# A fused LayerNorm, sliding-window attention and gated-FFN kernel: PV products per pair of head groups with resident attention weights and the first FFN weights on ScalarE's queue, in place of PV for four groups per run with streamed attention weights

## The chip, the cores and the metric

The kernel runs on one core of one Trainium2 chip. The metric is device time in microseconds for one launch of the whole program; the time before is the median of three runs.

## The reference, cut to what matters

```python
xn = (x - mean) / sqrt(var + 1e-5)                 # x: 1 x 2048 x 576, bf16
q, k, v = split(xn @ wqkv)                         # 32 heads of 18
mask = 0 <= i - j < 256                            # causal, window of 256
s = softmax(where(mask, q k^T * 18**-0.5, -1e9)) v # per head
s = s @ wo                                         # 576 x 576
h = sigmoid(xn @ w_gate) * (xn @ w_up)             # w_gate, w_up: 576 x 4608
g = h @ w_down                                     # 4608 x 576
out = x + s * silu(g)
```

## The kernel before, in words

The 2048 tokens are cut into four chunks of 512 (`NC = 4`), and each chunk into four blocks of 128 tokens. For a chunk the program normalizes x, brings it into the layout with features on partitions (`xnT`), projects V (`build_v`) and Q, K (`build_qk`, five column groups), does attention for eight head groups of four heads (`build_attn`), projects with `wo`, and does the FFN (`build_ffn`). The contraction over 576 features is 64 + 4 x 128; all matmuls use two halves of the array's rows, so they come in pairs that run side by side (`pair`, line 133).

In an attention step the scores of a head group fill five tiles ("bins") of 1024 columns. ScalarE takes exp of each into one slot of the ring `expr`, VectorE multiplies the mask blocks, and later a **PV run** (`f_pv` in `build_pv`, line 838) multiplies the weights with V. A PV run consists of matmuls that load 19 columns of V (18 and a column of ones for the softmax sum) and stream 64 to 320 columns; eight of them, four on the column groups times two on the row halves, run side by side. With `PVG = 2` a run serves four head groups: 192 matmuls (128 in chunk 0, which has no keys of an earlier chunk), eight runs in all. The `expr` ring has `NEX = 20` slots, which is what four head groups need. VectorE then transposes, divides by the sums and transposes back, and DMAs put the result in `oT`.

The attention weights are not kept: `load_qk` brings the columns of each Q/K group again in every chunk into a ring of two (`wqk`, `wqkr`), and `load_proj` brings `wv` and `wo` in turn into one buffer (`wvo`, `wvor`). The gate and up weights come from HBM in every chunk too, in 18 groups of two tiles of 128 hidden features, into a ring of four (`wgs`, rows 64 to 575) and a ring of two (`wgr`, the first 64 rows). `w_down` is loaded once.

The order on every engine is fixed when the program is built: `schedule` takes operations one after the other by estimated start and priority, so that FFN matmuls fill TensorE while attention steps wait for ScalarE and VectorE. TensorE executes its list in order. All loads are issued from SyncE (SP); the moves within SBUF from POOL and SP. `SPACE_NS` holds, for each chunk and head group, the distance in time that the planner keeps between the score tiles.

TensorE's list also contains waits. A matmul carries one semaphore wait itself; further ones stand in the list as instructions of their own. In `pad_pe` the program counts TensorE's instructions, compares the place of each PV run with a period of 256 instructions, and writes extra waits for something long done into the FFN steps ahead of it:

```python
            phase = (sizes[i][0] + added + PHASE) % HALF
            mid, lo = PV_PHASE[0], PV_PHASE[1] - PV_PHASE[0]
            need = 0 if (phase - mid) % HALF <= lo else (mid - phase) % HALF
```

At the start SyncE issues four loads of x, the first gate and up weights (`dma:w:0:0`), their first 64 rows, and then the next groups, while TensorE multiplies zeros (`warm`) and ScalarE loads its table (`init:tab`, line 481).

Of the kernel before, what the change touches and what calls it, by code (L numbers as in the profile page):

```python
# [36 lines left out]
NEX = 20  # L37
NWQ = 2
PVG = 2
# [15 lines left out]
          ((3, 1, 1, 2), (7, 1, 0, 1)), ((4, 1, 1, 2),))  # L55
NXN = 2
NST = 3
NQD = 1
NFIN = 2
NTH = 4  # L60
OT_PRIO = 1
EVAC = (1, 0)
NOT1 = 1
NOT2 = 1
NOT3 = 2
MK_PRIO = 1
# [15 lines left out]
HALF = 256  # L82
PHASE = 73
PV_PHASE = (80, 124)
WAITS_FREE = 2
# [11 lines left out]
SPACE_NS = ((2200, 1700, 1500, 1700, 1700, 1700, 1700, 2000),  # L97
            (1700, 2200, 1300, 1500, 2500, 1600, 1700, 900),
            (1600, 1200, 1700, 2000, 900, 1700, 1300, 1700),
            (2200, 1700, 1700, 2200, 1700, 2500, 1700, 700))  # L100
# [4 lines left out]
def mm_ns(n):  # L105
    return max(24.7, n / 2.4 + 2.7)
# [42 lines left out]
class Hold:  # L149

    __slots__ = ("pool", "n", "units", "rel", "parts")

    def __init__(self, pool, n):
        self.pool = pool
        self.n = n
        self.units = None
        self.rel = []
        self.parts = None
# [3 lines left out]

    def split(self):
        self.parts = [Hold(self.pool, 1) for _ in range(self.n)]
        return self.parts


class Pool:
# [27 lines left out]
    def take(self, hold, units):  # L196
        deps = []
        for u in units:
            if self.last[u] is not None:
                deps += self.last[u].rel  # L200
            self.last[u] = hold
        hold.units = units
        for u, part in zip(units, hold.parts or ()):
            self.last[u] = part
            part.units = [u]
        return deps
# [40 lines left out]


class Counter:

    def __init__(self):
        self.n = 0

    def matmul(self, *a, **k):
        self.n += 2

    transpose = matmul
# [22 lines left out]
class Builder:  # L280
# [38 lines left out]
    def alloc_memory(self):  # L319
# [30 lines left out]
        self.ot1, _ = seq("ot1", [P, NOT1, NT], f32)  # L350
        self.o2, _ = seq("o2", [P, NOT2, NT])
        self.o2T, _ = seq("o2T", [P, NOT3, NT])
        self.oT, _ = seq("oT", [P, KB, NT])
        self.s_attn, _ = seq("s_attn", [P, BPC, D])
        self.wqk, _ = seq("wqk", [P, NWQ, KB - 1, 2, P])
        self.wqkr, _ = seq("wqkr", [P, NWQ, P])
        self.wvo, _ = seq("wvo", [P, KB - 1, D])
        self.wvor, _ = seq("wvor", [P, D // 2])
        self.qd, _ = seq("qd", [P, NQD, 2, NT])
        self.xnr, _ = seq("xnr", [P, NXN, XW])  # L360
# [22 lines left out]
    def build_graph(self):  # L383
        self.r_xn = Ring(NXN, "xnr")
# [4 lines left out]
        self.r_wq = Ring(NWQ, "wqk")  # L389
        self.r_wvo = Ring(1, "wvo")  # L390
        self.r_ex = Ring(NEX, "expr")
        self.r_ot1 = Ring(NOT1, "ot1")
        self.r_o2 = Ring(NOT2, "o2")
        self.r_o2T = Ring(NOT3, "o2T")
# [20 lines left out]
        self.xn_slot = {}  # L415
# [23 lines left out]
    def load_x(self, c, i=0):  # L439
# [8 lines left out]
        for _ in range(2):  # L448
            s_, d_ = self.r_xn.produce()
            slots.append(s_)  # L450
            dd += d_
        assert slots[1] == slots[0] + 1
        o = self.dma(self.xnr[:, slots[0]:slots[0] + 2, RD:XW],
# [3 lines left out]
        for j in range(2):  # L457
            self.x_dma[st + j] = (o, self.xnr[:, slots[j], RD:XW])
            self.xn_slot[st + j] = slots[j]
# [9 lines left out]
    def build_consts(self):  # L469
# [15 lines left out]
        self.warm(NWARM[0], z, None, 107)  # L485

# [35 lines left out]
    def build_ln(self, c):  # L522
# [3 lines left out]
        for i in range(BPC):  # L526
# [24 lines left out]
            sn, dn = (self.xn_slot[st], []) if c else self.r_xn.produce()  # L551
# [16 lines left out]
            self.ln_dup = dup  # L568
            self.r_st.release(ss, ap)
# [56 lines left out]
    def load_proj(self, c, w, name):  # L626
        _, d = self.r_wvo.produce()
        o = [self.load_nat(self.wvo[:, :, :], w, f"dma:{name}:{c}", ("wvo",), 6, d)]
        o += self.load_rem(self.wvor[:, :], (w[:, 0:288], w[:, 288:D]), f"dma:{name}r:{c}", ("wvor",), 6, d)
        if c == 0:  # L630
            for x in o:
                x.slack = 5000.0
        return o

    def load_qk(self, c, gi):
        sw, d = self.r_wq.produce()
        n = P if gi < 4 else RD
        cols = [self.wqkv[:, i * D + gi * P:i * D + gi * P + n] for i in range(2)]
        o = []
        for i, w in enumerate(cols):  # L640
            dst = self.wqk[:, sw, :, i, :] if gi < 4 else self.wqk[:, sw, :, 0, i * RD:i * RD + RD]
            o.append(self.load_nat(dst, w, f"dma:wqk:{c}:{gi}", ("wqk", sw, i), 5, d))
        if gi < 4:
            o += self.load_rem(self.wqkr[:, sw, :], cols, f"dma:wqkr:{c}:{gi}", ("wqkr", sw), 5, d)
        else:
            for t in range(2):
                for i in range(2):
                    o.append(self.dma(self.wqkr[ROWS[t], sw, i * RD:i * RD + RD], cols[i][0:RD, :], 2 * RD * RD * 2,
                                      f"dma:wqkr:{c}:{gi}", ("wqkr", sw, t), deps=d, prio=5))
        if c == 0:  # L650
            for x in o:
                x.slack = 2500.0
        return sw, o

    def build_qk(self, c, gi):
        op = self.op
        sw, wdeps = self.load_qk(c, gi)
# [4 lines left out]

        def lhs(r, t, k):
            return self.wqk[r, sw, k - 1, 0 if gi == 4 else t, :] if k else self.wqkr[r, sw, :]
# [4 lines left out]
        pj = self.two("qk", f"{c}:{gi}", n, h, lhs, rhs, [self.op_xnT[c], wdeps, dq], n)  # L669
        self.r_wq.release(sw, pj)  # L670
# [44 lines left out]
    def build_v(self, c):  # L715
        op = self.op
        wdeps = self.load_proj(c, self.wqkv[:, 2 * D:3 * D], "wv")
        xs = c % 2
        for i in range(BPC):
# [5 lines left out]
            vp = self.row_proj("v", st, h, lambda r, k, cols=cols: self.xnT[r, xs, k, cols], self.wvo, self.wvor,  # L725
                               [self.op_xnT[c][i], wdeps, war])
            self.r_wvo.release(0, vp)
# [16 lines left out]
    def build_attn(self, c, hg):  # L744
# [21 lines left out]
        for vi, (specs, groups) in enumerate(zip(bins, masks)):  # L766
# [27 lines left out]
            for g0, ng, m0, m1 in groups:  # L794
# [10 lines left out]
                mk = op("DVE", dve_ns(2 * ng * (m1 - m0) * SW, 2.0), f_mk, f"mk:{c}:{hg}:{vi}:{g0}", deps=[ex, self.op_mask], prio=MK_PRIO)  # L805
# [6 lines left out]
        if hg % (2 * PVG) == 2 * PVG - 1:  # L812
            self.build_pv(c, hg // 2 - PVG + 1)

    def build_pv(self, c, pr):
        op = self.op
        pend, self.pend = self.pend, []
        hp = self.pool_s.hold(PVG)
        hps = hp.split()
# [5 lines left out]
        def f_pv(eng):  # L825
            res = None
            for u, n, ks in [(u, n, ks) for u in range(PVG) for n, ks in enumerate(kss)]:
                outs = self.halves(hps[u], NT)
                q0, q1 = span[ks]
                cols = slice(q0 * SW, q1 * SW)  # L830
                for g, (hg, where, _) in enumerate(pend[2 * u:2 * u + 2]):
# [10 lines left out]
        est = TURN_NS + PVG * sum(mm_ns((b - a) * SW) for a, b in span.values())  # L842
# [5 lines left out]
        for pr, hp, i in [(pr + u, hps[u], i) for u in EVAC for i in range(2)]:  # L848
# [6 lines left out]
            def f_t1(e, i=i, p1=p1, hp=hp):  # L855
                return e.transpose(self.ot1[:, p1, :], self.halves(hp, NT)[i])  # L856
            t1 = op("DVE", dve_ns(NT), f_t1, f"ot:{c}:{pr}:{i}", deps=[pv, d1], prio=OT_PRIO)
            hp.release(t1)
            rc = op("DVE", 255, lambda e, o1=o1: e.reciprocal(o1[:, :, DH], o1[:, :, DH]), f"rc:{c}:{pr}:{i}", deps=[t1], prio=OT_PRIO)
            on = op("DVE", dve_ns(NT // 32 * DH), lambda e, o1=o1, o2=o2: e.tensor_tensor(  # L860
                o2[:, :, 0:DH], o1[:, :, 0:DH], o1[:, :, DH:VH].broadcast_to([P, NT // 32, DH]), ALU.mult),
                f"on:{c}:{pr}:{i}", deps=[rc, d2, self.op_o2z], prio=OT_PRIO)
            self.r_ot1.release(p1, on)
            t2 = op("DVE", dve_ns(NT), lambda e, p2=p2, p3=p3: e.transpose(self.o2T[:, p3, :], self.o2[:, p2, :]),  # L864
                    f"ot2:{c}:{pr}:{i}", deps=[on, d3], prio=OT_PRIO)
# [8 lines left out]
        if pend[0][0] == 0:  # L874
# [17 lines left out]
    def build_wo(self, c):  # L892
        op = self.op
        wdeps = self.load_proj(c, self.wo, "wo")
        last = []
        for i in range(BPC):
# [7 lines left out]
            wo = self.row_proj("wo", qb, h2, lambda r, k, cols=cols: self.oT[r, k, cols], self.wvo, self.wvor,  # L904
                               [self.op_o[c], wdeps, war])
            self.r_wvo.release(0, wo)
# [217 lines left out]
    def schedule(self):  # L1124
# [14 lines left out]
        while nsched < len(ops):  # L1139
# [66 lines left out]
            for s_ in o.succs:  # L1206
# [8 lines left out]
                if remaining[s_.cidx] == 0 and s_.idx < 0:  # L1215
                    enabled[s_.eng].append(s_)
        self.prog = prog
# [4 lines left out]

    def waits_of(self, o, known):
        waits = {}
        for d in o.deps:
            k, v = d.tok
            if waits.get(k, -1) < v:
                waits[k] = v
        out = [(k, v) for k, v in waits.items() if known.get(k, -1) < v]
        known.update(out)  # L1230
        return out

    def pad_pe(self):
        known, at, sizes, free = {}, 0, [], {}
        prog = self.prog["PE"]
        for o in prog:
            cnt = Counter()
            nw = len(self.waits_of(o, known))
            extra = max(0, nw - WAITS_FREE)
            free[o] = max(0, WAITS_FREE - nw)  # L1240
            o.fn(cnt)
            sizes.append((at + extra, cnt.n))
            at += extra + cnt.n
        pads = {}
        added, first = 0, 0
        for i, o in enumerate(prog):
            if not o.name.startswith("pv:"):
                continue
            phase = (sizes[i][0] + added + PHASE) % HALF
            mid, lo = PV_PHASE[0], PV_PHASE[1] - PV_PHASE[0]  # L1250
            need = 0 if (phase - mid) % HALF <= lo else (mid - phase) % HALF
            hosts = [p for p in prog[first:i] if p.name.startswith("f")]
            for n, p in enumerate(hosts):
                k = need * (n + 1) // len(hosts) - need * n // len(hosts)
                if k:
                    pads[p] = k + free[p]
# [95 lines left out]
```

## Time and profile before

| | before |
|---|---|
| median of three runs | 575.99 us (575.91 to 576.23) |
| the profiled execution, its time | 576.23 us |
| its span, first to last instruction | 574.9 us |
| TensorE matmul busy | 556.7 us, 97% of the span |
| VectorE, ScalarE, POOL busy | 331.6, 273.6, 208.4 us |
| mean granted TensorE clock | 0.994 |
| DMA traffic | 75.90 MB, mean 132 GB/s |
| TensorE matmuls | 8342 |

The profiled execution took 1.3 us more than its span, and 0.24 us more than the median of the runs. Busy time of TensorE is that of pipelined matmuls with modelled ends; where it stands still is seen better in the chain of work that ended last, whose pieces the prediction shows.

### The profile page before, as it was taken

To read this page: it belongs to the slowest core of one execution; us is meant where nothing else is said; L and a number is where in the kernel's file an instruction comes from. 1 tells how busy PE (TensorE), PEld (TensorE's weight loads), DVE (VectorE), ACT (ScalarE), POOL (GpSimd) and SP (SyncE) were. 2 spreads that over 40 slices of the span, in tenths; PEclk is the share of its full clock that TensorE was granted. 3 is DMA by queue.
4 is the path that set the end of the run, shared out by engine and by line. 5 is a ranking of instruction groups with operands and counts; after the bars stand their busy time and mean duration, and the time that the engine had idled before them with its cause. 6 is when DMAs were issued, how large, how long until landed. Compare 5 with 4: busy or idle time off the path is not lost.

```text
span 574.9 us, 19878 instructions
## 1 busy us (share of the span) xinstructions
PE 556.7 (97%) x8342; PEld 359.3 (62%) x8342; DVE 331.6 (58%) x792; ACT 273.6 (48%) x383; POOL 208.4 (36%) x360
## 2 busy tenths in 40 slices
PE   8999997999999989999999999989998999999997
PEld 7565443888566544467775555546877755555687
DVE  4466664844867649656856675575263955642123
ACT  4245651443455645672556366534562567333111
POOL 5614441565442413554633355335141530110000
PEclk9999997999999999999999999999999999999999
DMA  8999896432177634752253376536321156271010
GB/s 224 250 289 241 232 229 193 124 72 67 35 174 221 182 109 121 200 145 53 47 144 108 91 192 167 166 100 160 87 76 35 26 149 179 72 205 47 3 43 23
DMA packets 141343, 75.90 MB, mean 132 GB/s; under 512 B 43804, under 2 KB 139388, under 8 KB 141256
## 3 DMA queue, kind: packets, MB, share of 16 engines
q1 hardware_dynamic: 133832, 68.71, 44.7%
q0 software_dynamic: 7424, 5.92, 3.9%
q8 instruction: 68, 1.11, 0.8%
q14 instruction: 19, 0.16, 0.1%
HBM read 63.18 MB, written 2.36 MB: 114 GB/s over the span
## 4 chain that ended last, share of the span: by engine, by line
PE 96%; issue 2%; DMA 1%; SPq 0%; DVE 0%; DVEq 0%
PE ps L133 92%; PE ps L838 3%; DMA wgs<-in_B_w_up_dram 1%; SPq L309 0%; DVE s_attn L1101 0%; DVE thf L1106 0%; PE ps L610 0%; DVE xf L1111 0%; DVEq L1299 0%
## 5 line engine op out<-in xcount | busy, mean ns | idle before, releaser
L133 PE MATMUL ps<-xnT,wgs 64*128 64x512 bf16 (+1 forms) x2400 | 288.8, 370 | 0.8 <-PE ps L133 0.5
L791 ACT ACTIVATE expr<-ps 128x1024 bf16<-128x1024 f32 (+4 forms) x160 | 154.8, 968 | 83.1 <-PE ps L133 82.4
L133 PEld LDWEIGHTS ps<-xnT,wgs 64*128 64x128 bf16 x2400 | 121.0, 94 | 110.2 <-issue 3.6
L133 PE MATMUL ps<-wd_sb,hT 64*128 64x288 bf16 (+2 forms) x2448 | 155.1, 276 | 0.0
L985 ACT ACTIVATE tring<-ps 128x512 bf16<-128x512 f32 x144 | 86.1, 598 | 136.9 <-PE ps L133 120.4
L988 DVE SCALAR_TENSOR_TENSOR hT<-tring,ps 128x512 bf16<-128x512 bf16 x144 | 98.6, 685 | 77.3 <-ACT tring L985 74.9
L133 PEld LDWEIGHTS ps<-wd_sb,hT 64*128 64x128 bf16 x2448 | 117.9, 94 | 23.7
L309 POOL DMA_DIRECT2D qk<-qd x160 | 81.7, 518 | 100.1 <-PE ps L133 55.5
L804 DVE TENSOR_TENSOR expr<-expr,mask 128x128 bf16<-128x128 bf16 (+2 forms) x240 | 64.6, 299 | 76.3 <-ACT expr L791 74.8
L309 POOL DMA_DIRECT2D oT<-o2T x72 | 36.9, 519 | 112.5 <-DVE o2T L864 91.6
L755 POOL TENSOR_SCALAR kx<-kprev,small 128x256 bf16<-128x256 bf16 x64 | 60.2, 951 | 40.1 <-PE ps L133 39.1
L133 PE MATMUL ps<-qk,kx 64*128 64x320 bf16 (+1 forms) x704 | 60.4, 254 | 0.0
L133 PE MATMUL ps<-xnT,wgr 64*128 64x512 bf16 (+1 forms) x300 | 57.3, 369 | 0.0
L133 PEld LDWEIGHTS ps<-qk,kx 64*128 64x128 bf16 x704 | 33.9, 94 | 23.3 <-ACT expr L791 1.1
L856 DVE STREAM_TRANSPOSE ot<-ps 128x512 f32<-128x512 f32 x32 | 22.4, 701 | 30.2 <-PE ps L838 29.9
L133 PE MATMUL ps<-xnT,wqk 64*128 64x512 bf16 (+1 forms) x320 | 38.0, 355 | 0.1
L1091 ACT ACTIVATE thf<-ps 128x576 bf16<-128x576 f32 (+3 forms) x22 | 11.4, 518 | 49.3 <-PE ps L133 49.0
L838 PE MATMUL ps<-expr,v_aug 64*19 64x320 bf16 (+4 forms) x1408 | 20.2, 255 | 12.8 <-issue 12.8
L838 PEld LDWEIGHTS ps<-expr,v_aug 64*19 64x19 bf16 x1408 | 17.2, 86 | 17.4 <-issue 15.6
L759 POOL COPY kprev<-qk 128x256 bf16<-128x256 bf16 x32 | 12.6, 400 | 38.2 <-DVE kx L755 36.9
L755 DVE TENSOR_SCALAR kx<-qk,small 128x512 bf16<-128x512 bf16 x64 | 21.7, 365 | 7.7 <-PE ps L133 4.4
L133 PEld LDWEIGHTS ps<-xnT,wgr 64*128 64x128 bf16 x300 | 16.1, 95 | 15.9 <-issue 0.5
(67 smaller groups left out, 305.8 us busy)
## 6 DMA issues: line engine op xcount, KB each, us to landing
wgs<-in_B_w_gate_dram SPq DMA_DIRECT2D x72, 256.0 KB, 3.6
wgs<-in_B_w_up_dram SPq DMA_DIRECT2D x72, 256.0 KB, 3.9
wd_sb<-in_B_w_down_dram SPq DMA_DIRECT2D x9, 576.0 KB, 6.4
wqk<-in_A_wqkv_dram SPq DMA_DIRECT2D x32, 128.0 KB, 3.1
qk<-qd POOLq DMA_DIRECT2D x100, 36.0 KB, 2.6
wgr<-in_B_w_gate_dram SPq DMA_DIRECT2D x36, 64.0 KB, 2.9
wgr<-in_B_w_up_dram SPq DMA_DIRECT2D x36, 64.0 KB, 3.1
wvo<-in_A_wqkv_dram SPq DMA_DIRECT2D x4, 576.0 KB, 4.6
```

The lines of the kernel that those rows point to most:

```text
L133: res = eng.matmul(outs[i], lhs(ROWS[t], i), rhs(ROWS[t], i), start=start, stop=stop, tile_position=(64 * t, 0))
L309: o = self.op(eng, DMA_ISSUE_NS[eng], lambda e: e.dma_start(dst, src), name, deps, prio, nbytes=nbytes)
L755: return e.tensor_scalar(self.kx[:, sx, pos:pos + n_ // SW, t, :], src.rearrange("p (s k) -> p s k", k=SW), self.half[:, t:t + 1], None, A ...
L759: self.op_kp[hg] = op("POOL", 420, lambda e: e.tensor_copy(self.kprev[:, hg, :], self.qk[:, qs, 1, NT // 2:NT]), f"kp:{c}:{hg}", deps=[kxo ...
L791: return eng.activation(self.expr[:, se, :, lo * SW:NT], self.both(h, NT)[:, :, lo * SW:NT], ACTF.Exp, scale=SM_SCALE)
L804: return eng.tensor_tensor(e_, e_, m_, ALU.mult)
L838: res = eng.matmul(outs[i][p0:p0 + VH, cols], self.v_aug[ROWS[i], o:o + VH], self.expr[ROWS[i], se, t, cols], start=n == 0, stop=n == len( ...
L856: return e.transpose(self.ot1[:, p1, :], self.halves(hp, NT)[i])
L985: th = op("ACT", act_ns(NT), lambda e: e.activation(self.tring[:, st, :], bank(h, 0), ACTF.Tanh, scale=0.5), f"th:{c}:{ft}", deps=[pg, dt_ ...
L988: mu = op("DVE", dve_ns(NT), lambda e: e.scalar_tensor_tensor(self.hT[:, ft, :], self.tring[:, st, :], 1.0, bank(h, 1), ALU.add, ALU.mult) ...
L1091: return e.activation(v2(t)[:, a:b, :], y2()[:, a:b, :], ACTF.Tanh, scale=0.25)
```

## The change

PV runs serve two head groups (96 matmuls, or 64 in chunk 0; sixteen runs), with an `expr` ring of 12 slots. All of `wqkv` and `wo` is loaded once and stays in SBUF (`wqk`, `wqkr`, `wv_sb`, `wo_sb` and their remainders); the last 64 columns of Q and K are copied together by VectorE (`wq4`). x of later chunks has its own ring (`xr`), `qd` has two slots in place of one. The extra waits on TensorE (`pad_pe`) are gone, `SPACE_NS` has other values. After the order is made, the two loads of the first gate/up weight group are taken out of SyncE's list and put into ScalarE's behind the operation that loads its table; all x loads stay on SyncE.

```diff
-NEX = 20
-NWQ = 2
-PVG = 2
+NEX = 12
...
+NXR = 2
...
-NQD = 1
+NQD = 2
...
-HALF = 256
-PHASE = 73
-PV_PHASE = (80, 124)
-WAITS_FREE = 2
...
+        wq, wk, wv = (self.wqkv[:, i * D:(i + 1) * D] for i in range(3))
+        self.op_wqk = [self.load_nat(self.wqk[:, :, i, :], w, "dma:wqk", ("wqk", i), 5) for i, w in enumerate((wq, wk))]
+        self.op_wqk += self.load_rem(self.wqkr[:, :], (wq, wk), "dma:wqkr", ("wqkr",), 5)
...
+        self.op_wv = [self.load_nat(self.wv_sb[:, :, :], wv, "dma:wv", ("wv",), 6)]
...
+        self.op_wqk4 = [op("DVE", 420, lambda e: e.tensor_copy(self.wq4[:, 1:KB, :, :], self.wqk[:, :, :, 512:D]), "init:wq4",
+                           deps=self.op_wqk, prio=2)]
+        for t in range(2):
+            for i in range(2):
+                self.op_wqk4.append(op("DVE", 130, lambda e, t=t, i=i: e.tensor_copy(
+                    self.wq4[ROWS[t], 0, i, :], self.wqkr[ROWS[1 - i], 512:D]), f"init:wq4:{t}{i}", deps=self.op_wqk, prio=2))
...
     def build_qk(self, c, gi):
         op = self.op
-        sw, wdeps = self.load_qk(c, gi)
...
     def build_v(self, c):
         op = self.op
-        wdeps = self.load_proj(c, self.wqkv[:, 2 * D:3 * D], "wv")
...
         self.pend += [(hg, where, ready)]
-        if hg % (2 * PVG) == 2 * PVG - 1:
-            self.build_pv(c, hg // 2 - PVG + 1)
+        if hg % 2:
+            self.build_pv(c, hg // 2)
+        if (c, hg) == (0, 1):
+            pv = self.op_pv[(c, hg)]
+            self.op_wo_w = [self.load_nat(self.wo_sb[:, :, :], self.wo, "dma:wo", ("wo",), 8, [pv])]
...
         def f_pv(eng):
             res = None
-            for u, n, ks in [(u, n, ks) for u in range(PVG) for n, ks in enumerate(kss)]:
-                outs = self.halves(hps[u], NT)
+            outs = self.halves(hp, NT)
+            for n, ks in enumerate(kss):
...
+        first = [o for o in prog["SP"] if o.name == "dma:w:0:0"]
+        for o in first:
+            prog["SP"].remove(o)
+            o.eng = "ACT"
+            o.deps.append(self.op_tab)
+        at = prog["ACT"].index(self.op_tab) + 1
+        prog["ACT"][at:at] = first
...
-    def pad_pe(self):
...
-                for _ in range(pads.get(o, 0)):
-                    eng.wait_ge(self.sem["DVE"], 1)
```

## The prediction, made before the changed kernel ran

> **What bounds the kernel now.** I read the busy shares first: TensorE has 97% of the span, the next engine 58%. So only what TensorE does or waits for counts. The chain of waits in order of time (start, length, what) shows where its time is not work:
>
> ```profile
> 10.54 77.12 PE ps L133 x804
> 87.65 1.69 PE ps L838 x110
> 89.34 3.28 issue
> 92.62 0.54 PE ps L838 x16
> ...
> 209.12 1.55 PE ps L838 x106
> 210.67 2.43 issue
> 213.10 1.02 PE ps L838 x64
> ...
> 216.24 45.69 PE ps L133 x554
> 261.93 2.45 PE ps L838 x167
> 264.38 55.20 PE ps L133 x808
> ```
>
> Outside the PV runs (line 838) TensorE flows for tens of microseconds without a hole. Inside a PV run it stops once, and waits for "issue": nothing that the profile shows. Seven of eight runs have such a stop; the one at 261.93 has none. TensorE's own waits (total, times, longest) show that nothing else is of that size; no load and no other engine holds it for more than 1.0 us:
>
> ```profile
> PE ps L838 <- issue: 12.8, 7, 3.3
> PE ps L133 <- DVE small L480: 1.0, 1, 1.0
> PE ps L133 <- PE ps L133: 0.5, 3, 0.2
> PE ps L610 <- DVE xnr L558: 0.4, 1, 0.4
> PE ps L133 <- DMA wgs<-in_B_w_up_dram: 0.3, 1, 0.3
> ```
>
> What releases the stops? The table of queues (packets, MB, share) has one of kind "instruction":
>
> ```profile
> q8 instruction: 68, 1.11, 0.8%
> ```
>
> That is 16 KB a packet. TensorE's list has 2 x 8342 instructions for matmuls and their weight loads and 753 waits of their own, 17,438 with one more: 68.1 times 256, so a packet is a block of 256 TensorE instructions. I counted through the built program's list up to the first matmul after each stop: it has number 2496, 4288, 6081, 9665, 11201, 13505 and 15041, each time 192 or 193 above a multiple of 256. The stop is the end of a block whose successor has not come. By the trace's packet times TensorE resumes 1.26 to 1.51 us after a packet of q8 has landed, and a packet's fetch begins, late in the kernel, about when TensorE enters the block before. A block of FFN work takes about 11.5 us, so its successor is there in time; a PV run eats 384 instructions in 2.45 us.
>
> How long a successor needs, counted from the entry into the block ahead of it, is shown by the seven blocks that ended in a stop: 7.18, 3.63, 4.79, 3.08, 4.13, 3.52 and 2.62 us, and at most 2.20 us for the run without a stop. The first is in chunk 0, where the DMA share is highest.
>
> One more thing hangs on the first stop. The stages after 86 us (length, TensorE busy and count, the same of PEld, DVE, ACT and POOL, granted clock, DMA share, GB/s):
>
> ```profile
> 86.00:87.50 1.50, 1.50 (x16) 0.55 (x12) 0.87 (x3) 1.33 (x3) 1.46 (x3) 1.00 1.27 237
> 87.50:93.10 5.60, 2.32 (x130) 1.66 (x129) 0.65 (x1) 0.00 (x0) 0.88 (x1) 0.88 1.13 324
> 93.10:99.00 5.90, 5.74 (x31) 1.94 (x30) 4.17 (x8) 0.60 (x1) 0.00 (x0) 0.53 0.33 109
> ```
>
> After the longest stop the granted clock is 0.53 for 5.9 us.
>
> **The change part by part.** *PV runs of half the length.* What a stop costs I take from whole runs. The unstopped run takes 2.45 us. The other five of chunks 1 to 3 take 5.00, 3.29, 4.99, 4.33 and 3.48 (their pieces in the chain), 8.84 us above 5 x 2.45. The two of chunk 0 (5.51 and 3.41) stream three quarters of the columns, so 1.90 us without a stop, and are 5.12 above. Together 13.9 us. The clock: from 93.10 to 99.00 run 28 matmuls of 512 columns; eight of them take 0.86 us before the stop, so 3.0 us at full clock, 2.9 less than they took, of which 0.24 is a wait between the two halves of one FFN tile. That leaves 2.65 us.
>
> These 16.5 us are there to be had. A run in the new kernel has 192 instructions, so a block holding one entirely has 64 others, and those are slow: eight down-projection matmuls take 0.49 us, 31 ns an instruction; ten gate/up matmuls 1.08 us, 54 ns. I walked through the changed program's list for each run's place in its block. Eleven runs begin 110 to 231 instructions after a block's start, so they are cut in two, with many slow instructions in both blocks; these blocks take 5 us and more, against 2.2 to 4.8. Five are almost whole in one block: the second of chunk 0 begins 4 instructions after the block's start, the last of chunk 1 at 35, the first three of chunk 3 at 5, 17 and 33. A run itself will take about 1.4 us (half the unstopped run, and its own start). With 64 others of 31 ns, as at 17 and 33, the block takes 3.4 us; with 54 ns, as at 5 and 35, 4.6 to 4.8. In chunk 0 (128 instructions in the run, 128 of 46 ns on average around it) it takes 7.1. Against the mean delay of the later stops, 3.6 us, two blocks stop for 0.2 us each; with the scatter up to 4.8, 1.4 each, and the chunk-0 one 0.1. I take 1.0 us in all; the ends are 0 and, if all five meet the longest delay and some f2 block mixed with scores is shorter still, 5.5.
>
> *Eight more starts of a run.* Before the run at 261.86 the last sixteen FFN matmuls need 1.07 us instead of 0.98: 0.09 for the switch. The run streams 5120 columns, 2.15 us at the rate of the gate/up pairs (0.42 ns a column), and lasts 0.31 longer. What of this is paid anew in each run, and what goes with the number of matmuls, the trace does not show: 0.09 to 0.40 a run. I take the middle, 0.25: 2.0 us, ends 0.7 and 3.2.
>
> *Resident attention weights.* SP loses 102 of 112 issues (40 wqk, 48 wqkr, 8 wvo, 16 wvor become 10), and 7.8 of 10.4 MB are not moved. TensorE waits for no load after 8 us, so this is worth nothing on the path, and the cover is the whole queue of FFN work. Where it could cost: in chunk 0 the whole of wqk, wqkr and wv, 1.9 MB, now stand on SP ahead of weight group 4. At the 290 GB/s of the first slices they hold it back 6.5 us, to about 21; group 4 is used after eight FFN tiles and four Q/K passes of 0.9 us, at about 27. If that cover were gone, the price would be the lateness, once. The five copies for wq4 are some 1.2 us of VectorE (0.38 for the nearest large row, 0.20 for a small one), beside a VectorE that is 58% busy.
>
> *The ring of 12, the second qd slot, the x ring, the new spacings.* Ten slots serve a pair of groups, so the third score tile of the next pair waits for the PV run. In the new list that tile stands behind the run, and TensorE, which runs its list in order, waits for itself only. Masks must be ready for a PV run earlier than before, as two groups and not four are collected; TensorE's list puts FFN steps between. The trace has 0.24 us for a hole of that kind, three times; I take no change, and 0 to 2 us for the upper end.
>
> *No extra waits.* 533 instructions leave TensorE's list (753 become 220 waits). They cost nothing while the weight load runs ahead; they made blocks end sooner.
>
> *The first weights from ScalarE.* Now SP issues four x loads until 2.61, then gate 2.65 to 3.08 and up 3.13 to 3.64; the up weights land at 7.67 and the first FFN matmul starts at 7.81. ScalarE's table operation ends at 2.29, so gate starts at about 2.35 and up at about 2.85: 0.3 us sooner. On SP the issues behind move up by 1.0 us. On ScalarE the statistics of the third x block wait behind the two issues, until about 3.4; they wait for x until 4.46 anyway. The activation that brings the first block into xnT ends at 7.06 and TensorE's second transpose at 7.57, so no more than 0.3 can be had. I take 0.3; ends 0.6 gained and 0.3 lost, if both queues' packets share the engines and the up half comes no sooner.
>
> [...]
>
> **The sum.** 576.2 (the profiled execution, span 574.9) - 13.9 - 2.65 + 1.0 + 2.0 - 0.3 = 562.3; the median is 0.24 below the profiled execution, so 562.1, and I say 562. The ends: 576.0 - 16.5 + 0.7 - 0.6 = 559.6 and 576.0 - 16.5 + 5.5 + 3.2 + 0.3 + 2 = 570.5, which needs all bad ends at once; two thirds of the way up is 568.
>
> **The rivals.** *The stop belongs to the run, not to the block.* If each PV run stops once whatever its length, 13.9 / 8 = 1.74 us a run, sixteen cost 27.8: 576.0 + 13.9 + 2.0 - 0.3 = 591.6 with the clock loss as now. It decides against the change where the mean stop of the new runs is over (16.5 - 1.7) / 16 = 0.93 us. For it: seven of eight runs have one. Against it: the one without, and the numbers modulo 256. 5%.
>
> *The fetch is later than in the blocks I took.* If delays of 5 to 7 us, as in chunk 0, were met in chunks 1 to 3 too, some eight blocks would stop, for 6 to 12 us: 567 to 574. For it: the 7.18. Against it: none of the later ones is over 4.8, and less DMA traffic remains. 10%.
>
> *The new order has holes of its own*, in chunk 0's loads or at masks: the same 567 to 574, 3%. *The loads on ScalarE bring nothing:* 562.3, within the forecast.
>
> **How the numbers follow.** My forecast, 559 to 567, has 82%; the later or larger stops 13%; the rival above 576, 5%. The range 559 to 568.5 leaves some 15% out. 0.2% (1.2 us) is about what can be told from no change here. Faster by more: 0.94; within: 0.02; slower: 0.04.
>
> **What would show it.** Right: sixteen PV pieces in the chain, most unbroken at about 1.4 us, issue waits at line 838 under 3 us in all, granted clock 1.00 at 90 to 100 us, first FFN matmul near 7.5. Wrong: a stop in most runs, or TensorE waiting for wgs, expr or hT at line 133.

## The result and the profile after

The changed kernel takes 559.84 us (559.55 to 560.22), against 575.95 us before (the median of four runs now): a ratio of 0.9725 (95% interval 0.9708 to 0.9741), some 16 us less. The forecast was 562 us, with a range of 559 to 568.5.

The chain of waits of the changed kernel, in order of time (start, length, what; line 801 is now the PV run, line 122 the other matmuls):

```profile
65.02 0.94 PE ps L801 x64
65.96 22.02 PE ps L122 x228
87.97 0.94 PE ps L801 x64
88.91 23.44 PE ps L122 x288
...
407.58 1.27 PE ps L801 x90
408.85 17.22 PE ps L122 x294
426.07 1.27 PE ps L801 x89
427.34 12.86 PE ps L122 x218
```

The whole chain has sixteen PV pieces, four of 0.94 us in chunk 0 and twelve of 1.27 us after it, none with a stop. (The counts of such a piece are lower than the 96 matmuls of a run, since matmuls that overlap are merged in the chain.) The stage that ran at half clock before, and the queue of instruction blocks together with the new queue of ScalarE (packets, MB, share):

```profile
93.10:99.00 5.90, 5.90 (x64) 2.75 (x60) 5.34 (x14) 3.94 (x5) 2.64 (x6) 1.00 0.43 117
```

```profile
q8 instruction: 66, 1.08, 0.8%
q10 hardware_dynamic: 1056, 0.52, 0.3%
```

The clock there is 1.00, and TensorE is busy all through. The matmuls in the stretch are not the same ones; eight of 512 columns take 1.03 us, where they took 1.89 at half clock (0.50 granted from 91.80 to 98.63 us in the trace before). What is left of TensorE's waits (total, times, longest) and the place of the one that is new:

```profile
PE ps L122 <- DVE small L451: 1.0, 1, 1.0
PE ps L122 <- issue: 0.9, 1, 0.9
PE ps L599 <- DVE xnr L545: 0.8, 1, 0.8
```

```profile
10.61 0.11 PE ps L122 x3
10.72 0.89 issue
11.61 12.79 PE ps L122 x166
```

The new stop of 0.89 us is not in a PV run but at the very start, among the first FFN pieces; the first matmul after it is instruction 449 of the built list, again 193 above a multiple of 256. It is the only stop at a block's end in this execution, and the forecast did not have it.

### The profile page after: what moved, and what is told of

The parts are those of the page before. It is cut to its first block, busy times and chain, and to the rows that moved or that the text cites. A ratio compares the mean times of both kernels' runs of the same rounds, so it can differ in the third digit from the quotient of the medians.

```text
span 558.9 us, 19261 instructions
## 1 busy us (share of the span) xinstructions
PE 552.9 (99%) x8342; PEld 339.8 (61%) x8342; DVE 333.8 (60%) x797; ACT 274.2 (49%) x383; POOL 210.0 (38%) x360
## 3 DMA queue, kind: packets, MB, share of 16 engines
HBM read 55.15 MB, written 2.36 MB: 103 GB/s over the span
## 4 chain that ended last, share of the span: by engine, by line
PE 98%; DMA 1%; DVE 0%; issue 0%; SPq 0%; ACT 0%; POOL 0%; DVEq 0%
PE ps L122 94%; PE ps L801 3%; DMA x<-in_A_x_dram 1%; PE ps L599 0%; SPq L279 0%; ACT tring L586 0%; DVE s_attn L1062 0%; POOL small L533 0%; DVE xnr L541 0%; DVE thf L1067 0%; DVE xf L1072 0%; POOL small L587 0%; DVE xnr L545 0%; DVEq L1234 0%
## 5 line engine op out<-in xcount | busy, mean ns | idle before, releaser
L122 PE MATMUL ps<-xnT,wgs 64*128 64x512 bf16 (+1 forms) x2400 | 282.7, 368 | 1.0 <-issue 0.9
L122 PEld LDWEIGHTS ps<-xnT,wgs 64*128 64x128 bf16 x2400 | 114.1, 94 | 115.6 <-DVE hT L949 1.6
L122 PE MATMUL ps<-wd_sb,hT 64*128 64x288 bf16 (+2 forms) x2448 | 156.7, 276 | 0.0
L122 PEld LDWEIGHTS ps<-wd_sb,hT 64*128 64x128 bf16 x2448 | 112.7, 94 | 28.2
L764 DVE TENSOR_TENSOR expr<-expr,mask 128x128 bf16<-128x128 bf16 (+2 forms) x240 | 63.3, 298 | 61.9 <-ACT expr L751 61.4
L122 PEld LDWEIGHTS ps<-qk,kx 64*128 64x128 bf16 x704 | 31.2, 94 | 21.5 <-ACT expr L751 0.6
L122 PE MATMUL ps<-xnT,wqk 64*128 64x512 bf16 x256 | 32.6, 376 | 0.0
L1052 ACT ACTIVATE thf<-ps 128x576 bf16<-128x576 f32 (+3 forms) x22 | 11.4, 518 | 39.7 <-PE ps L122 39.4
L827 DVE STREAM_TRANSPOSE o2T<-o 128x512 bf16<-128x512 bf16 x32 | 22.7, 711 | 1.0
L637 DVE CAST qd<-ps 128x1024 bf16<-128x1024 f32 (+1 forms) x20 | 22.1, 1111 | 1.5 <-PE ps L122 1.5
L697 ACT ACTIVATE v_aug<-ps 64x288 bf16<-64x288 f32 x32 | 13.1, 408 | 17.3 <-PE ps L122 16.8
```

What stands on the lines that cost most here:

```text
L122: res = eng.matmul(outs[i], lhs(ROWS[t], i), rhs(ROWS[t], i), start=start, stop=stop, tile_position=(64 * t, 0))
L637: return eng.tensor_copy(dst, self.both(h, n))
L697: return eng.activation(dst, src, ACTF.Copy)
L764: return eng.tensor_tensor(e_, e_, m_, ALU.mult)
```

## The experiments

Three questions were open after the result: is it the block or the run that stops, do the resident weights carry a part of the gain, and where does the stop at the start come from.

### Long runs at other places in their blocks

Two kernels keep the long runs of before and change only the extra waits. One counts the waits as the built list has them: a matmul carries one wait itself, the others stand two to an instruction (at the shifted start below, 128 of them are 64 records in the trace).

```diff
-PHASE = 73
-PV_PHASE = (80, 124)
-WAITS_FREE = 2
+EDGE = 193
+PV_AT = (128, 72)
...
+            size.append(cnt.n + max(0, nw) // 2)
...
+                need = (want - (start - EDGE)) % HALF
...
+                        pads[prog[p]] = 2 * (nws[p] // 2 + k) - nws[p]
```

> The kernel before, with its eight long PV runs, but the extra waits ahead of each run are counted as the built list has them, so that a run begins 128 instructions after a block's start in chunk 0 and 72 (once 89) in chunks 1 to 3; a run is then cut into two nearly equal parts by a block's end. Block theory (the stop is the end of a block of 256 instructions whose successor has not come): most stops go or shrink; the shortest blocks are about 2.5 us for two runs amid down-projection matmuls (about 1.1 us of stop each at the mean delay of 3.6 us), 3.3 us for one, 3.9 us and more for the rest. Sum of stops 2 to 4 us, granted clock 1.00 at 93 to 99 us, time 576.0 - 13.9 - 2.65 + 3 = 562.5 us (561 to 564). Run theory (a run of more than some 105 matmuls stops once wherever it stands, a short one does not): stops of 1.5 to 2 us in seven or eight runs, 574 to 577 us.

Measured: 565.54 us (ratio 0.9828, 0.9761 to 0.9894). Six of the eight long runs have no stop. The chain shows an unbroken one, whose 2.40 us are all 192 matmuls, and the one with the longer stop of the two others:

```profile
203.82 2.40 PE ps L837 x164
206.22 2.07 PE ps L132 x17
...
428.02 1.24 PE ps L837 x86
429.26 1.54 issue
430.81 1.42 PE ps L837 x93
```

The run at 428 stands amid down-projection matmuls, one of the two that were expected to stop; its stop is after 92 of 192 matmuls, at the block's end, where it was after 152 before. The other run stops for 0.5 us, and two stops of 0.4 and 0.3 us stand behind a run, each at a block's end too: 2.8 us in all, as expected. So the length of the run does not make the stop, and the run theory is out. The time is 1.5 us above the range given. In the traces the first PV run starts at 89.27 us, against 87.65 in the kernel before, which has 600 wait instructions fewer, and 87.16 in the next kernel, which has no extra waits: the further ones are not free at the start (below).

The other kernel leaves the extra waits out:

```diff
-        pads = self.pad_pe()
+        pads = {}
```

> The kernel before without its extra waits on TensorE; nothing else differs. The long runs then begin 157, 251, 237, 254, 233, 132, 223 and 253 instructions after a block's start. Block theory: the third run pair's second run (the one at 132, chunk 2) has no stop, as its block's end cuts it in two; the first run (157) has none or under 1 us; the other six stop by 3.6 less 1.5 us, some 2 us each, at the instruction that ends a block, so after about 128 to 142 matmuls of the run. Stops 10 to 16 us in all, no loss of clock, time about 573 us (569 to 577). Run theory: all eight stop, 1.74 us each on average, after 105 to 152 matmuls wherever the block ends; 576 us.

Measured: 574.44 us (ratio 0.9965, 0.9925 to 1.0005). There are seven stops, 11.4 us in all. Six are in runs, and the seventh is the clearest evidence of all. Two places of the chain:

```profile
134.81 1.79 PE ps L838 x124
136.60 0.23 PE ps L133 x2
136.82 1.31 issue
138.13 63.82 PE ps L133 x740
...
366.97 2.38 PE ps L838 x160
369.35 2.48 issue
371.83 0.22 PE ps L838 x2
```

The run at 134.81 was to stop and did not. Its stop comes 0.23 us behind it, in FFN matmuls of line 133, at the end of a block of which the run fills the first 251 instructions: the run starts 5 instructions ahead of the block and has 256. The stop belongs to the instruction count, wherever that falls. The run at 366.97 was expected to have none, and has one of 2.48 us: my count was at fault. Starting 132 instructions into its block, a run of 384 meets a block's end after 124 instructions and again after 380, with a whole block of PV between; the stop stands at the second, with the last four instructions of the run still to come.

### Short runs with streamed weights

```diff
-PVG = 2
+PVG = 1
-EVAC = (1, 0)
+EVAC = (0,)
...
-        pads = self.pad_pe()
+        pads = {}
```

> The kernel before with PV runs of two head groups and without the extra waits; the attention weights are still loaded anew in each chunk, the ring of exp results keeps 20 slots, and all first loads are on SyncE. Block theory, and nothing to be had from resident weights: no stop, or one or two of up to 0.5 us, DMA traffic as before (75.9 MB); time 559 to 561 us, that of the changed kernel within 1 us. If the resident weights carry a part of the gain: 564 us or more, with TensorE waiting for wqk or wvo.

`EVAC` lists the pairs of head groups whose results are copied out after a run; with one pair it has one entry.

Measured: 561.36 us (ratio 0.9762, 0.9696 to 0.9828). No PV run stops, with all attention weights still loaded in every chunk. Most of the change's gain is thus had by two constants and the removal of the waits. TensorE has no wait for `wqk` or `wvo`. The time is 0.4 us above the range expected and 2.4 us above that of the kernel with short runs, resident weights and SyncE loads (below). Its chain shows a part of this as stops at block ends soon after a run:

```profile
440.36 1.27 PE ps L838 x90
441.64 1.18 PE ps L133 x18
442.82 0.59 issue
443.41 14.80 PE ps L133 x154
```

This run began 27 instructions into its block, so the block holds it whole and ends 37 instructions behind it, in the down projection. The packet of the block behind it began 1.1 us after TensorE had entered the block. Such short stops were expected in the changed kernel as well, which had none. What is left of the 2.4 us after this one and another of 0.44 us was not taken apart: the order of the steps, the spacings, the ring sizes and the loads differ together, and the two were measured on different chips.

### The first loads: which queue

Beside the changed kernel stands one that differs from it only in the queue of the first two weight loads:

```diff
-        first = [o for o in prog["SP"] if o.name == "dma:w:0:0"]
-        for o in first:
-            prog["SP"].remove(o)
-            o.eng = "ACT"
-            o.deps.append(self.op_tab)
-        at = prog["ACT"].index(self.op_tab) + 1
-        prog["ACT"][at:at] = first
```

> The changed kernel as it is, beside the next three on the same chip: 559.8 us, no stop in a PV run, one stop of about 1 us near 10.5 us.

> The changed kernel with its first two gate/up loads left on SyncE; nothing else differs. If the second queue costs (the fetch of the block at instruction 449 comes 1.6 us later with it): the first FFN matmul at about 7.8, no stop at 10.5, the FFN tile at 15.59 us starts at 14.8, time 559.84 - 0.8 = 559.0 us. If the stop comes from the other loads: it stays, and the time is 559.9 to 560.2 us, as the first FFN matmul is 0.1 us later.

Measured: 559.85 us (559.35 to 562.71) and 558.97 us (558.70 to 559.36). The same pair again, run apart:

> The changed kernel once more: 559.8 us, a stop at instruction 449 of 1 to 2.8 us with the fetch begun at 9 to 10 us.

> The kernel with short runs, resident weights and the first gate/up loads on SyncE, beside the next two on the same chip: 559.0 us. Its first look had a stop of 0.6 us at instruction 449 with the block's fetch begun at 8.39 us; the long-run kernels with all loads on SyncE began it at 7.3 to 7.6. If that is scatter from run to run: a start between 7.3 and 8.4 us and a stop of 0 to 0.6 us.

Measured: 560.13 us (559.29 to 560.41) and 559.13 us (558.71 to 559.41). The second queue costs 0.9 and 1.0 us of the median. The FFN tile that tells the start's end, which begins at 14.82 us in the kernel before and at 15.59 in the changed one, begins at 18.05 and 15.21 us in the two further traces of the changed kernel and at 14.64 and 14.67 with the loads on SyncE. In the first pair the profile of the changed kernel has the longest stop seen at the start, that of the kernel with the loads on SyncE a short one:

```profile
PE ps L122 <- issue: 2.6, 1, 2.6
```

```profile
10.13 0.11 PE ps L122 x3
10.24 0.42 issue
10.66 12.80 PE ps L122 x166
```

In the second pair the changed kernel stops for 0.8 us, less than expected, and the other not at all. The five traces of these two kernels show the chain of causes: the packet's fetch began at 10.20, 8.99, 8.53, 8.39 and 8.32 us, and the first matmul of the new block came 1.34 to 1.43 us after the packet had landed, at 12.74, 11.61, 11.23, 10.66 and 10.69. The 2.6 us stop is followed by 3.41 us at half clock, which makes that execution the slowest of its six, 562.71 us.

The same part of the change alone in the kernel before:

> The kernel before with the one other part of the change alone: the first two gate/up loads issued from ScalarE behind its table load. As forecast: first FFN matmul 0.3 us sooner, 575.7 us. By the changed kernel's trace (first FFN matmul 0.12 us sooner, but TensorE stands 1.1 us at instruction 449, the end of its first full block, whose successor's fetch began at 8.99 instead of 7.38 us): the same stop of about 1 us near 10.5 us, the FFN tile that starts at 14.82 us before starts 0.8 us later, 576.8 us. If that late fetch comes from the new kernel's other loads, no stop.

Measured: 577.44 us, ratio 1.0014 (0.9971 to 1.0057). The time decides nothing, since the kernel before scatters over 9 us in these runs. The trace does: the packet's fetch began at 8.82 us instead of 7.38, and TensorE stands 0.8 us in issue within the third transpose. The matmul after this stop has number 448 in the list, 192 above a multiple of 256, so this is the block's end that was expected to stop. The FFN tile starts at 16.16 us instead of 14.82, 1.3 us later where 0.8 was expected; the rest is a longer wait for the normalized x, `xnr` (1.0 us instead of 0.4). The stop thus comes with the second queue, without any other part of the change. Two variants ask whether a lighter second queue is harmless:

```diff
-        first = [o for o in prog["SP"] if o.name == "dma:w:0:0"]
+        first = [o for o in prog["SP"] if o.name == "dma:wgr:0:0"]
```

> The changed kernel with the first group's two loads of 64 rows (64 KB each) on ScalarE in place of the two of 256 KB. If the late fetch is a matter of the bytes that stand ahead of it, 128 KB instead of 512 KB on the second queue leave the fetch at about 7.4 to 8 us: no stop or under 0.3 us at instruction 449, 559.1 us. If any second queue does it: the stop of 1 us stays, 559.9 us.

Measured: 559.80 us (559.28 to 561.36). There is no stop at instruction 449, yet the tile that tells the start's end begins at 16.32 us. TensorE waits 0.8 us for the first block of `xnT`, and the profiled execution has 3.41 us at half clock just there (granted clock, third number from the end):

```profile
8.34:11.75 3.41, 3.33 (x69) 3.37 (x71) 0.99 (x10) 0.77 (x2) 2.35 (x4) 0.50 1.02 266
```

So TensorE came late to the block's end, after a fetch that began at 8.67 us, and this trace cannot say whether lighter loads remove the stop. The time is that of the changed kernel; two of the six executions have a clock of 0.997, and the other four took 559.28 to 559.91 us.

The other is shown against the kernel with the loads on SyncE:

```diff
+        first = [o for o in prog["SP"] if o.name in ("dma:x1", "dma:x3")]
+        for o in first:
+            prog["SP"].remove(o)
+            o.eng = "ACT"
+        prog["ACT"][0:0] = first
```

> As the kernel with the first gate/up loads on SyncE, but the second and fourth x load are issued from ScalarE ahead of its table load, so that SyncE issues the first weights about 0.9 us sooner. If the start is bound by issue time: first FFN matmul at about 7.4 us (the statistics of x are ready no sooner), 0.3 to 0.5 us gained, 558.6 us. If the late fetch comes with any second queue of loads: a stop of about 1 us near 10.5 us as in the changed kernel, 559.5 to 560 us.

Measured: 559.48 us (558.97 to 560.18): no gain over 558.97, 0.5 us worse. Its trace has no stop at instruction 449 and the tile at 14.54 us, so neither account holds, and the profiled executions of the two kernels, 559.18 and 559.20 us, do not show where the 0.5 us are lost. Over all traces but that of the shifted start (below) the fetch of the block for instruction 449 began at 7.3 to 8.4 us where all loads are on SyncE, at 8.1 with x loads shared, and at 8.5 to 10.2 us with weights on ScalarE. With weights on ScalarE it is later in every trace, but 8.39 and 8.53 nearly touch, and something else moves the fetch as well: with all loads on SyncE it began at 7.3 to 7.6 us where the attention weights are streamed and at 8.3 to 8.4 where they are resident. By what way loads hold back the packets of q8 was not shown.

### The start shifted in its block

The kernel with the loads on SyncE gets 64 wait instructions ahead of TensorE's first matmul and less warm-up:

```diff
-NWARM = (43, 10)
+NWARM = (37, 10)
...
+                for _ in range(128 if o.name == "warm:0" and e == "PE" and not known else 0):
+                    eng.wait_ge(self.sem["DVE"], 1)
```

> The same kernel with 64 waits for something long done (as 64 instructions) ahead of TensorE's first instruction and 6 of the 43 first warm-up pairs less, so that 40 more instructions stand ahead of the first transpose and every later instruction stands 40 places further in its block. TensorE enters its first fetched-ahead block some 0.7 us sooner, in the warm-up. Block theory: that block's fetch is begun sooner by about as much, the block's end is reached in the FFN piece before the third transpose, and the stop there stays at 0 to 0.6 us; the PV runs move to 217, 44, 248, 159, 15, 198, 183, 75, 199, 240, 202, 150, 45, 57, 73 and 192 after their block's start and none stops by more than 0.7 us. 558.5 to 559.3 us. If the waits delay the warm-up, the clock rises later and the first FFN matmuls run slow: 559.5 to 561.

Measured: 564.31 us (ratio 0.9798, 0.9767 to 0.9830), outside both expectations. TensorE's first matmul comes at 7.95 us, where it was at 1.05:

```profile
7.95 1.36 PE L122 MATMUL ps<-hT 64*128 64x128 bf16 x22 [7.95 <-DVE xnr L545]
```

The releaser that is named is not what held it. The waits are for VectorE's first operations, which end at 1.00 us, and the trace has a record of each of the 64 wait instructions, two waits in each: they start at 1.03 to 7.84 us, 0.106 to 0.146 us apart, so 0.108 us each on average. The question of the start was not answered by this kernel, but its sixteen runs at new places in their blocks all ran without a stop.

## Why the prediction was right, point by point

The mechanism was the one forecast: the stops at block ends and the clock loss behind them are gone. That 562 us came within 2.2 us of the measured time is in part luck: the start cost 1.1 us more than forecast, while the stops kept for the new runs (1.0 us), the net of old stops and new starts (0.9 us) and the holes of the old order (1.4 us) came out better.

**The stop is the end of a block.** Right. Long runs stop or not by their place (six of eight without a stop when placed), a stop falls outside the PV run when the block ends there, and none falls into a short run in any of the six kernels that have them. What the old stops cost is gone entirely. It was a little more than the 13.9 us: the placed long runs take 2.40 us without a stop, and 1.79 in chunk 0, where I had taken 2.45 and 1.90. That makes 18.0 us for eight runs, which last 32.5 us in the chain of the kernel before, so the stops come to 14.5 us. The 1.0 us that I kept for the new runs was not needed, because the packets behind the two tightest blocks came early. In the trace those blocks, with the runs at 407.5 and 426.0 us, take 3.19 and 3.17 us, and their successors had landed 2.8 and 2.1 us before their ends; in the six other traces of this list it was 1.8 us or more. In the kernel of streamed weights the same kind of block did stop, for 0.59 us. Why the packet came early in the one and late in the other is not shown.

**The clock.** The 2.65 us of the profiled execution came back. But it was one execution's price. Thirty runs of the kernel before, made beside these experiments, order themselves by the mean granted clock: 571.3 to 573.5 us at 1.000 (6 runs), 573.7 to 574.8 at 0.997 (4), 575.8 to 577.3 at 0.994 (5), 577.5 to 579.6 at 0.991 (12), 579.3 to 580.5 at 0.988 (3). A step of 0.003 is one period of 3.41 us at half clock (the trace before has 6.83 us of it, at 0.994), and the runs are about 2 us longer with each. Eleven more on a third chip go the same way with more scatter: 572.6 to 575.9 us at 0.996 and 0.997 (3), 574.8 to 577.5 at 0.993 and 0.994 (6), 578.0 and 578.8 at 0.991 (2). By the clock the kernel before has between none and four such periods, and most of its scatter goes with them; the changed kernel's own runs for the result lie within 0.7 us.

**Eight more starts of a run.** Right. The pieces add up to 12 x 1.27 + 4 x 0.94 = 19.0 us, against 6 x 2.40 + 2 x 1.79 = 18.0 for the long runs without a stop, plus 8 x 0.09 for the switch: 1.7 us, 0.22 a start, where I took 0.25. By the prediction's own 18.5 us for the long runs it would be 1.2 us.

**Resident weights.** Forecast at nothing. Short runs with streamed weights are 2.4 us slower than the kernel that also has its first loads on SyncE, and 1.0 us of that is stops at block ends; whether the weights are worth a part of the other 1.4 us stays open.

**The first weights from ScalarE.** This step failed. Forecast: 0.3 us gained, because SyncE's issue time stood in the way. The loads were issued at 2.32 and 2.79 us, as worked out, and the first FFN matmul started at 7.69 instead of 7.81. What was late next was a packet that I had left out of the account: the block that begins at instruction 449. It was fetched from 8.99 to 10.25 us, among the first loads, and TensorE was at the end of the block ahead of it at 10.72. The term is not -0.3 but +0.9 us, and the best kernel of the study is the changed one without it: 558.97 and 559.13 us.

**No extra waits.** I took these as free. In the traces the tile that ends the start begins at 14.34 us without them, at 14.82 in the kernel before and at 16.13 with the 600 further ones; where nothing covered them, at the shifted start, 64 cost 0.108 us each. Amid FFN work they were free: a stretch of 846 matmuls takes 59.51 us in the kernel before, with 164 separate waits ahead of its PV run since the last one, and 59.51 us without the extra waits, with 27.

**The sum.** Profile against profile, 576.2 - 560.2 = 16.0 us. The terms as measured give 14.5 + 2.65 - 1.7 - 0.8 (the tile that ends the start, at 15.59 instead of 14.82) = 14.6. The other 1.4 us lie elsewhere in the order: 0.9 of them at the score tiles, whose 704 matmuls take 34.1 us before and 33.2 after, from each one's start to the next one's. The rest was not traced. I had put the new order at no change.

In these traces the crossing from one block to the next cost TensorE nothing wherever the block lasted longer than 5.1 us, and a stop in every block shorter than 2.2 (six in the kernel before, with stops of 0.72 to 2.43 us); in between both were seen, the start's stop among them (a block of 4.9 us and a stop of 0.89 in the changed kernel). The half clock came with the stop of 3.28 us in the kernel before, and for 3.41 us behind one of 2.48 us (the run at 366.97 without extra waits); the two of 2.43 and 2.36 us in the kernel before had none behind them.

## What to carry to other kernels

When an engine that is busy nearly always stands still in "issue", count its instructions to the first one after each stop. Here the numbers agreed modulo 256, the stop was a block of instructions that came late, and it went when no block was made of fast instructions alone: from all sixteen runs with shorter stretches of them, from six of eight with other places. Count in the built list, not in the source, since waits are put together there; and do not shift places with waits where no work covers them, where 64 of them took 6.9 us. Before a second queue is given to the first loads, look at what else is fetched in those microseconds, the instructions among it: here the second queue cost 0.9 to 1.0 us.

## What was not expected of the hardware

- Wait instructions that had nothing to wait for took 0.108 us each on TensorE where no work covered them: 64 of them moved the first matmul from 1.05 to 7.95 us.
- Half-clock periods followed stops of 2.43, 2.48 and 2.58 us, not only the one of 3.28, and not each time: by the mean clock the kernel before has none to four of them in executions that do the same work, 571.3 to 580.5 us. One stop of 2.43 us is in two traces of the same TensorE list. In the kernel before, full speed follows it (1.02 us for the rest of the run, 2.07 for 17 matmuls); with the first loads on ScalarE, half clock does:

```profile
210.69 2.43 issue
213.11 1.56 PE ps L838 x64
214.67 3.16 PE ps L133 x14
```

- With the first weights on a second queue the fetch of the next block of instructions began at 8.5 to 10.2 us, without it at 7.3 to 8.4, and the stop that follows varied from none to 2.6 us with it and from none to 0.4 without.
